# A list schedule with a model of the port that VectorE and GpSimd share, a table of shifts on its priorities, later constants, fewer weight tiles decoded early

## The chip, the core and the metric

The kernel runs on one NeuronCore of a Trainium2 chip. Its engines are TensorE (PE in the profile; PEld is its loading of weights), VectorE (DVE), ScalarE (ACT), GpSimd (POOL) and SyncE (SP), which here issues nearly all DMAs. The metric is the device time of one execution in microseconds (us), as the median of several runs.

## The reference

Three blocks follow one another: causal attention with a decay made from a cumulative sum of log f, a gated feed-forward block with a convolution of width 3 along the sequence, and a Fourier mixing block with a feed-forward network.

```python
# attention: B, H, S, D = 4, 8, 576, 64
cum = np.cumsum(np.log(np.clip(f, 0.0001, 1.0)), axis=-1)
scores = scale * q @ k.T + cum[..., :, None] - cum[..., None, :]     # causal, then softmax
x = softmax(scores) @ v                                              # -> (B, S, 512)
# gated block, d_ff = 1024
h = np.maximum(x @ w_in, 0.0)
conv_out = sum(conv_w[k] * hp[:, k:k + S, :] for k in range(3))      # hp: h padded
x = h * sigmoid(conv_out) @ w_out
# mixing block, hidden width 2048
u = x + np.real(np.fft.fft(np.fft.fft(x, axis=1), axis=2))
un = (u - mean(u)) / np.sqrt(var(u) + 1e-06)
out = u + np.maximum(un @ w_ch1, 0.0) @ w_ch2
```

## The kernel before

Everything is fp32. Where precision is wanted at the speed of float32r, a tensor is kept as a high part (ScalarE copies it to float32r) and a low part (GpSimd or VectorE subtracts, a tensor_tensor), and a product is three matmuls. The weights of the three feed-forward matrices arrive as 64-bit numbers and are decoded to fp32 on the chip: one DMA, an absolute value on ScalarE, a clamp on GpSimd (tensor_scalar) and three bit instructions on VectorE, each over 128x512 (`decode`).

The program is recorded first and ordered afterwards. `build` calls the engines' methods, and each call becomes an `Op` with an engine, a modelled cost in ns (`cost_of`), its predecessors and a priority. `Plan.order` then runs a list schedule over all operations forward (`forward`) and backward (`backward`) in turns; the backward run gives the next priorities, and the best of 40 forward runs is taken. `walk` does the scheduling: each engine takes the ready operation of the lowest priority number. The result is one fixed order of instructions for each engine's queue. In the forward run, TensorE's cost doubles in a stretch of 3413 ns whose predecessor had little work in it, and each DMA occupies a modelled wire. A VectorE instruction of over 32 elements with no PSUM operand is charged `1.25 * c + 60`, whatever GpSimd does.

What is recorded, with tile names as the profile has them:

- Attention, steps s = 0 to 16, two heads a step: scores into PSUM (psatt_s), VectorE adds the mask (att_t, att_nb), ScalarE takes the exponential, TensorE transposes (psatt_u, att_pt), the sums' reciprocals go through DRAM and come back spread over the partitions (att_r, att_rt, att_rb), and the product with v is scaled by them (att_xr), and split into bc_xs. The v tiles are att_tv.
- The gated block of each batch is queued when its 4 steps are through, and filled in between the attention's steps: 8 chunks x @ w_in with the convolution on VectorE (glu_cv__157 and glu_cv__158, three 128x576 instructions a chunk), then 16 chunks with w_out, whose tiles come from DRAM into two buffers (bc_wo__133, bc_wo__134). The result goes to DRAM as z (dram_t__341 to 344, one for each batch).
- The DFT of each batch (dft_*, psdft) reads z and the constant matrices dd (dft_t__3762) and ds (dft_t__3763). These are staged: GpSimd's queue copies the inputs in_dd and in_ds to dram_t__379 and dram_t__380 as float32r by four DMAs, not before a time `hold` in the plan (`1e4 * SCST` ns, 160 us); `load_consts` then loads them from there on SP.
- The last feed-forward block runs in eight passes over four groups of rows and eight groups q of the hidden width, each with the weights of a slot k = q % 5 (mr_*, ml_t, bc_*; products in psc_c). It needs w_ch1 and w_ch2 in 16 tiles each. `NST` of each are decoded during the attention (steps x = 10 on) and stored to DRAM (dram_t__347 on, two for a tile number fo); the rest stand in the list `todo`, of which `decode_some(2)` takes two a step in the third and fourth pass. `stored` loads a decoded tile back (wprep_dw), and `load_pair` makes a slot's weights from four of them: q = 4, the fifth slot, from fo = 8 and 9, in the third pass. All these tiles go through rings of two buffers (wprep_dr, wprep_dw, wprep_de).

An instruction's line in the profile is that of the emitter, so tiles tell the instructions apart, not lines.

Of the kernel before, what the change touches and what calls it, by code (L numbers as in the profile page):

```python
# [200 lines left out]

ENGINES = ("PE", "DVE", "ACT", "POOL", "SP")
# [53 lines left out]
    return n * 0.9 + 30.0  # L256


class Plan:
# [1192 lines left out]
```

## Time and profile before

| | us |
|---|---|
| median of 3 runs (867.5 to 869.25) | 868.6 |
| the profiled execution | 873.15 |
| its span, from the first to the last instruction | 871.4 |
| TensorE busy | 828.5 (95%) |
| VectorE busy | 652.9 (75%) |
| ScalarE busy | 430.2 (49%) |
| GpSimd busy | 250.7 (29%) |

The profile is of one execution. Busy time counts an engine's instructions; neighbours in one queue can overlap a little. The windows give the same for a stretch of the span, with the clock that TensorE was granted in it (1.00 is 2.4 GHz, 0.50 is 1.2 GHz) and the mean share of time in which the 16 DMA engines were busy. The timeline puts instructions in order of time; in square brackets stands an engine's idle time before the instruction and what ended it. A wait for several things is put down to the one that came last.

### The profile page before, as it was taken

What the parts mean: (1) busy time and instruction counts of PE and PEld (TensorE: products, weight loads), DVE (VectorE), ACT (ScalarE), POOL (GpSimd) and SP (SyncE); (2) the same over time, 40 slices, a digit from 0 to 9 for tenths busy, and PEclk for the clock granted to TensorE, in tenths of its full rate; (3) what the DMA queues carried; (4) which work ended last, traced back from release to release, by engine and by line L of the source; (5) the groups of instructions that cost most, each with busy time, mean ns of one, the idle gap of its engine ahead of it and who ended that gap; (6) DMA issues with size and microseconds to landing.
All of it is one profiled execution on the core that took longest, in us unless ns stands there. A gap on an engine that the chain in (4) does not pass through costs nothing.

```text
span 871.4 us, 15330 instructions
## 1 busy us (share of the span) xinstructions
PE 828.5 (95%) x5424; PEld 719.2 (83%) x5424; DVE 652.9 (75%) x1596; ACT 430.2 (49%) x1043; POOL 250.7 (29%) x271
## 2 busy tenths in 40 slices
PE   8999998799999999989899999999999999999998
PEld 6667777588978888889789788988998889899896
DVE  6988989745896598238867767786787888887754
ACT  5988787545775385236534434344432452323220
POOL 2243535400351133229945541232012220000000
PEclk9999999999998999999989999999999999999999
DMA  6464465978446923696886845423265623443222
GB/s 219 152 199 143 156 206 155 326 216 282 133 140 174 316 74 103 207 310 165 203 231 168 205 135 125 142 78 121 87 182 122 178 78 107 118 122 98 73 74 84
DMA packets 97804, 139.61 MB, mean 160 GB/s; under 512 B 17048, under 2 KB 59832, under 8 KB 97728
## 3 DMA queue, kind: packets, MB, share of 16 engines
...
q0 software_dynamic: 576, 2.95, 0.9%
...
## 4 chain that ended last, share of the span: by engine, by line
PE 66%; DVE 15%; DMA 6%; ACT 6%; issue 3%; POOL 3%; SPq 1%; DVEq 0%; ACTq 0%; POOLq 0%
PE psc_c__4874 L511 9%; PE psc_c__4873 L511 9%; PE psbc_bc__556 L511 6%; PE psbc_bc__557 L511 6%; PE psdft_x__3869 L511 4%; PE psdft_x__3870 L511 4%; PE psc_c__5047 L511 4%; PE psc_c__5046 L511 3%; PE psc_c__5045 L511 3%; PE psc_c__5044 L511 3%; DVE glu_cv__158 L511 3%; PE psatt_s__170 L503 3%; DVE glu_cv__157 L511 3%; PE psatt_u__174 L503 2%; PE psatt_u__174 L511 2%
## 5 line engine op out<-in xcount | busy, mean ns | idle before, releaser
L511 ACT ACTIVATE bc_xs__131<-ml_t__5369 128x320 fp32r<-128x320 f32 (+1 forms) x78 | 35.1, 450 | 98.4 <-DVE ml_t__5369 L511 87.3
L511 PE MATMUL psbc_bc__556<-bc_xs__131,bc_wi__130 128*128 128x288 f32 x384 | 62.8, 302 | 1.8 <-ACT glu_t__138 L511 0.8
L511 PE MATMUL psbc_bc__557<-bc_xs__131,bc_wi__130 128*128 128x288 f32 x384 | 62.1, 301 | 0.5 <-DVE glu_t__140 L511 0.5
L511 DVE TENSOR_TENSOR ml_t__5369<-psc_c__4874,ml_t__5369 128x320 f32<-128x320 f32 (+1 forms) x91 | 40.9, 461 | 26.2 <-PE psc_c__4874 L511 25.2
L511 DVE TENSOR_TENSOR ml_t__5369<-psc_c__4873,ml_t__5369 128x320 f32<-128x320 f32 (+1 forms) x91 | 41.0, 461 | 25.4 <-PE psc_c__4873 L511 23.0
L511 PEld LDWEIGHTS psbc_bc__556<-bc_xs__131,bc_wi__130 128*128 128x128 f32 x384 | 53.2, 188 | 3.7 <-ACT glu_t__139 L511 1.0
L511 PEld LDWEIGHTS psbc_bc__557<-bc_xs__131,bc_wi__130 128*128 128x128 f32 x384 | 54.6, 190 | 1.2 <-DVE glu_t__140 L511 0.7
L511 POOL TENSOR_SCALAR wprep_dw__125<-wprep_dw__125 128x512 f32<-128x512 f32 x24 | 17.9, 748 | 104.5 <-ACT wprep_dw__125 L511 104.4
L511 DVE SCALAR_TENSOR_TENSOR bc_xs__131<-ml_t__5369,bc_xs__131 128x320 fp32r<-128x320 f32 (+1 forms) x78 | 38.8, 499 | 10.6 <-ACT bc_xs__131 L511 10.2
L511 POOL TENSOR_SCALAR wprep_dw__122<-wprep_dw__122 128x512 f32<-128x512 f32 x24 | 16.6, 691 | 73.2 <-ACT wprep_dw__122 L511 73.1
L511 DVE COPY glu_t__140<-psbc_bc__557 128x256 f32<-128x256 f32 (+2 forms) x48 | 9.9, 261 | 35.4 <-PE psbc_bc__557 L511 31.9
L511 DVE SCALAR_TENSOR_TENSOR glu_cv__157<-glu_t__138,bc_cw__132,glu_cv__157 128x576 f32<-128x576 f32 x32 | 32.7, 1021 | 1.4 <-ACT glu_cv__157 L511 1.2
L511 DVE SCALAR_TENSOR_TENSOR glu_cv__158<-glu_t__139,bc_cw__132,glu_cv__158 128x576 f32<-128x576 f32 x32 | 31.3, 979 | 2.8 <-ACT glu_cv__158 L511 2.7
L511 ACT ACTIVATE glu_t__140<-psbc_bc__556 128x256 f32<-128x256 f32 (+2 forms) x48 | 8.5, 251 | 45.6 <-PE psbc_bc__556 L511 40.8
L511 ACT ACTIVATE ml_t__5371<-ml_t__5369 128x320 fp32r<-128x320 f32 (+1 forms) x26 | 11.7, 449 | 35.1 <-DVE ml_t__5369 L511 29.0
L503 PE MATMUL psatt_s__171<-att_t__67,att_t__66 64*128 64x288 f32 (+2 forms) x48 | 26.6, 553 | 0.0
L503 PE MATMUL psatt_s__170<-att_t__67,att_t__66 64*128 64x288 f32 (+2 forms) x48 | 26.1, 545 | 0.0
L503 PE MATMUL psatt_u__174<-att_pt__101,att_tv__92 128*64 128x448 f32 (+3 forms) x80 | 21.6, 417 | 1.7 <-ACT att_pt__102 L511 1.6
L503 PE MATMUL psatt_s__172<-att_t__67,att_t__66 64*128 64x288 f32 (+2 forms) x48 | 21.8, 460 | 0.0
L503 PE MATMUL psatt_s__173<-att_t__67,att_t__66 64*128 64x288 f32 (+2 forms) x48 | 21.7, 459 | 0.0
L503 PE MATMUL psatt_u__174<-att_pt__102,att_tv__93 128*64 128x448 f32 (+3 forms) x80 | 21.6, 417 | 0.0
L503 PE MATMUL psatt_s__170<-att_qk__70 64*128 64x288 f32 (+2 forms) x48 | 19.1, 484 | 1.8 <-DVE att_nb__95 L511 1.8
...
## 6 DMA issues: line engine op xcount, KB each, us to landing
wprep_dr__124<-in_moe_w_ch_dram SPq DMA_DIRECT2D x16, 512.0 KB
wprep_dr__121<-in_moe_w_ch_dram SPq DMA_DIRECT2D x16, 512.0 KB, 5.2
bc_wo__133<-dram_t__340 SPq DMA_DIRECT2D x13, 512.0 KB, 4.2
bc_wo__134<-dram_t__340 SPq DMA_DIRECT2D x13, 512.0 KB, 4.1
...
dram_t__346<-mr_us__4906 SPq DMA_DIRECT2D x18, 256.0 KB, 3.6
```

What stands on the lines that cost most here:

```text
L503: getattr(eng[op.eng], f)(**{k: v.real() if isinstance(v, View) else v for k, v in kw.items()})
L511: getattr(eng[op.eng], op.fn)(**kw)
```

## The change

Four things change. `SCST` goes from 16 to 30: the copies of dd and ds are recorded 7 steps later and held to 300 us of the plan instead of 160. `NST` goes from 10 to 8: 8 tiles of each matrix are decoded during the attention, and fo = 8 and 9 of both join the head of `todo`, which grows from 12 to 16. In the forward run a VectorE operation that `two_reads` picks out (no PSUM operand, over 32 elements, neither memset nor reciprocal) is charged its bare cost, and if a GpSimd tensor_tensor is running when it starts, 0.8 of what is left of that. And `order` runs 53 rounds, takes the last one's priorities, whatever span they gave, and adds to each a number of the table SHIFT: 7577 letters, one for an operation in the order of recording, each standing for -31 to +31 us of the plan's time (a lower number goes first).

```diff
-NWO, NST = 2, 10
+NWO, NST = 2, 8
...
-SCST = 16
+SCST = 30
...
+ROUNDS = 53
+LETTERS = "ABCDEFGHIJKLMNOPQRSTUVWXYZabcdefghijklmnopqrstuvwxyz0123456789+-"
+SHIFT = """
+BSSSSzeZSZ89LigeKBR0aZhwnRmwGp--4-+6++mq-s06+-F-8-6u-alusvgW+66w8ulcpbqmiXV+RBCsuVT+UXRzudhlCz99-BsL23wSPSJBIX
...
+"""
...
+def two_reads(fn, kw):
+
+    v = [x for x in kw.values() if isinstance(x, View)]
+    if fn in ("memset", "reciprocal") or "PSUM" in [x.t.slot.pool.space for x in v]:
+        return False
+    return max(x.free() for x in v) > 32
...
+            o.pair = o.eng == "DVE" and two_reads(o.fn, o.kw)
...
+            if o.eng == "POOL" and o.fn == "tensor_tensor":
+                port.append((t, t + o.took))
+            elif o.pair:
+                o.took = (o.cost - 60.0) / 1.25
+                for a, b in port[-8:]:
+                    if a <= t < b:
+                        o.took += (b - t) * 0.8
+                        break
...
-        best = None
-        for k in range(self.rounds):
-            span = self.forward(prio)[0]
-            if best is None or span < best[0]:
-                best = (span, prio)
+        for _ in range(ROUNDS):
+            self.forward(prio)
             prio = self.backward()
-        self.span, out = self.forward(best[1])
+        for i, c in enumerate("".join(SHIFT.split())):
+            prio[i] += 1e3 * (LETTERS.index(c) - 32)
+        self.span, out = self.forward(prio)
```

## Rows read from the trace of the kernel before

**Rows 1.** The page's parts 1 and 4: busy time, and shares of the last chain.

```profile
PE 828.5 (95%) x5424; PEld 719.2 (83%) x5424; DVE 652.9 (75%) x1596; ACT 430.2 (49%) x1043; POOL 250.7 (29%) x271
...
PE 66%; DVE 15%; DMA 6%; ACT 6%; issue 3%; POOL 3%; SPq 1%; DVEq 0%; ACTq 0%; POOLq 0%
```

**Rows 2.** The view of the cores: span in us, mean granted TensorE clock.

```profile
core 0: 871.4 us, clock 0.982
```

**Rows 3.** Windows: length, busy us of each engine (instructions), granted clock, DMA share, GB/s.

```profile
160.00:180.00 20.00, 14.17 (x99) 12.06 (x100) 10.79 (x30) 6.94 (x24) 3.89 (x4) 0.83 0.90 312
0.00:160.00 160.00, 146.98 (x1103) 110.96 (x1103) 142.07 (x435) 128.43 (x358) 66.09 (x83) 0.98 0.57 178
220.00:345.00 125.00, 119.68 (x898) 108.34 (x900) 101.27 (x203) 82.28 (x198) 41.99 (x34) 0.97 0.49 158
300.00:340.00 40.00, 38.86 (x298) 35.90 (x297) 35.83 (x60) 30.75 (x71) 13.55 (x11) 1.00 0.33 103
400.00:500.00 100.00, 92.19 (x584) 83.12 (x583) 76.28 (x154) 48.77 (x97) 65.25 (x72) 0.95 0.76 195
500.00:870.00 370.00, 365.13 (x2044) 323.96 (x2042) 279.12 (x658) 126.22 (x262) 51.49 (x55) 1.00 0.40 114
```

**Rows 4.** TensorE's waits by what ended them: us, times, longest; 29 rows in all.

```profile
PE psbc_bc__556 L511 <- DMA bc_wo__134<-dram_t__340: 5.1, 1, 5.1
...
PE psdft_x__3877 L511 <- DVE dft_ue__3776 L511: 0.2, 1, 0.2
```

**Rows 5.** Timeline: GpSimd's copies, SP's load, the matmul [idle before it and who ended it].

```profile
157.29 1.26 POOL L511 DMA_DIRECT2D dram_t__379<-in_dd_dram  x2
...
160.63 0.73 SPq L511 DMA_DIRECT2D bc_wo__134<-dram_t__340  x1
...
172.24 0.85 PE L511 MATMUL psbc_bc__556<-glu_t__145,bc_wo__134 128*128 128x288 f32 x2 [5.09 <-DMA bc_wo__134<-dram_t__340]
```

**Rows 6.** DMA issues: count, KB each, median us to landing.

```profile
bc_wo__134<-dram_t__340 SPq DMA_DIRECT2D x13, 512.0 KB, 4.1
...
dram_t__346<-mr_us__4906 SPq DMA_DIRECT2D x18, 256.0 KB, 3.6
```

**Rows 7.** Timeline of VectorE, then of GpSimd, around 316 us: start, length.

```profile
314.93 1.91 DVE L511 SCALAR_TENSOR_TENSOR wprep_dw__122<-wprep_dr__121,wprep_dw__122 128x512 int32<-128x512 int32 x1
...
316.76 0.81 DVE L511 SCALAR_TENSOR_TENSOR glu_cv__157<-glu_t__138,bc_cw__132,glu_cv__157 128x576 f32<-128x576 f32 x1
...
317.49 0.61 DVE L511 CUSTOM_DVE_ANT_0 att_t__84<-psatt_s__170,att_t__65 128x448 f32<-128x448 f32 x1
...
314.86 1.42 POOL L511 TENSOR_TENSOR glu_t__150<-glu_cv__158,glu_t__142 128x576 fp32r<-128x576 f32 x1 [2.34 <-issue]
...
316.80 1.24 POOL L511 TENSOR_SCALAR wprep_dw__125<-wprep_dw__125 128x512 f32<-128x512 f32 x1 [0.51 <-ACT wprep_dw__125 L511]
```

**Rows 8.** VectorE's groups by form, 0 to 500 us: count, busy us, mean ns, idle before.

```profile
L511 DVE SCALAR_TENSOR_TENSOR glu_cv__157<-glu_t__138,bc_cw__132,glu_cv__157 128x576 f32<-128x576 f32 x32 | 32.7, 1021 | 1.4 <-ACT glu_cv__157 L511 1.2
...
L511 DVE SCALAR_TENSOR_TENSOR glu_cv__158<-glu_t__139,bc_cw__132,glu_cv__158 128x576 f32<-128x576 f32 x32 | 31.3, 979 | 2.8 <-ACT glu_cv__158 L511 2.7
...
L511 DVE SCALAR_TENSOR_TENSOR glu_cv__158<-glu_cv__158,glu_t__139 128x576 f32<-128x576 f32 x16 | 15.9, 993 | 3.7 <-ACT glu_cv__158 L511 3.5
...
L511 DVE SCALAR_TENSOR_TENSOR wprep_dw__125<-wprep_dr__124,wprep_dw__125 128x512 int32<-128x512 int32 x18 | 15.9, 885 | 0.1
...
L511 DVE SCALAR_TENSOR_TENSOR wprep_dw__122<-wprep_dr__121,wprep_dw__122 128x512 int32<-128x512 int32 x14 | 13.0, 931 | 0.2
```

**Rows 9.** Timeline of SP, then TensorE, around 590 us.

```profile
561.96 0.47 SPq L511 DMA_DIRECT2D wprep_dr__124<-in_moe_w_ch_dram  x1
...
587.56 0.32 SPq L511 DMA_DIRECT2D dram_t__369<-wprep_dw__125  x1
...
592.70 0.32 SPq L511 DMA_DIRECT2D wprep_dw__122<-dram_t__365  x1
...
600.10 0.31 PE L511 MATMUL psc_c__4873<-bc_wi__130,ml_t__5378 128*128 128x320 f32 x1
```

More of the change, by code (lines that the diff above doesn't have):

```diff
@@ new lines @@
+TFBBBFBBBBBBBOBBBFBWSDWBBYeCFLCBbHTLIWSFFLCGUHBECVJCFTBRLEECFYFHFBBBCBDBSJPFJBCIDheZ2oU-FIQf1DCCEWFRNRFJy1vBg+
+4S7aFBQncC6BCD6TSSHBBBmILfBBBQCG0BDBBTB3UGoqlY5BCRlnv+OVIIFLnUhZjEKggbdcpgdpYsqbmtshrqutqt439Yp--VNdXUIRmkebqc
+6+qT1+x+foRQhWz1i7B63358wbGHEjOMpjjXbTYNOVPUJgFJefYYHGVeNYoQuiiWviVWaUeehgkmkXlfVirfdcBJCNo3995rmGlbRv30m4sCxs
+07yehhrpjvfeLWeSrdu-eJNBNJYXcSuWHBGr--J--9c-x5--+-0y89--WlmuusbjgnCs85lonsaelr2HkfIGNNGG420qMZOObfQJEQVJELEbcT
+YWZk8+Zihwhfga1sHTQDBBJzZWatjfrLTOUtVtuXPZesSGXaaYWQLQLNhSSDBBl-sq9-pT2mb+Kxg+gr+TVHqxi+OQBxix0VdSeXUfUiHBB36-
@@ new lines @@
+v8+-8--zz+894+8890SMTVQPGaIBBDGeMBLSCBIGBlaEUd401HbpDBCGPRVHMNMRBDFRIIwBH-IXJeYsBQCGcCEcKJ0ez1qDcLSSUEDEBBGHFG
+JGaKCUhcBOMyJwqeJ2YjVOOUTJ770BBBBBBCCCBBGLMNTCDJBZKBC-DDfJYSS3BBz+v0-GQNSNegafcYVPhPMbgLo-dBEtEY0PGJDZq75nEBJK
+WQHCBBBCBBBBBBBBBBDBBBBCDJNBBBCBCFYFBBBDDBDcMCB755EJDEaQUYnbEDWp7giDUVOENbaEdOagd1ih0hNu-sluoRXXWfYocgamOCDDDD
+QVHBBCFFBLGRFFBHCDGFDDDHEJy7qkcUCBDEFBBBI3-neBNIZX8pZZGu4N41zvLD2x-zz1533-g4KLC+-c6IJIjhHhDBRp35uDBNYHNTKdQYKG
+INELFGhnNNwor83ku-GlSmmkOmROOTYGdLELMUeEBLClvBh72moMLKK---uBCCoy88fBBBCCBCYBJPiGQXVedRVGJBBBCDBCKHPBIJNuNKU99B
@@ new lines @@
+cBBICBBHJJHOHHNKKIhHHHHHOLTJLWM5XIILCBBBBHFBHJNIQSgaBBiFLkIRCFFHCDDBBNFBBFWPlqoCELgTcwUUTRhsmhBtUNCCLGIGDgHDI1
+immsqZFrbIcvgtWNGNIMJLdJLUWULLIHIahYUReeidiiaYeklHfwFROGQsBgjepWOHEEBC6IOTWYYFHEGIaRSBLFBFgCBBDBBBFUeKPDDPBJFG
+BNBBFPKYPQWHZlYo0ut-+5+----9---9v-gQoIGFKFGMQF3HBBBBhWBHBEFBKBbcBBBBBBFBDBDNCBBcKCSKx-w5GBBbgbhfnjj4zx1xhpPgtg
+1WNfgalwdZBBCCFQHI-3-9UurEMFbt253yMXCLPbTTv231-6J2++6+5vo-EYs3pq8nNsNOlZZIBei1peIBBOBBBBBBBBBBCLBeN-+-dZ4zFCet
+9--nWZpaarZWatjjiqSypFgpt889Tn38BN2fCBkoiGNaSMBBH-kolFZI2QzUX7ejj4TUhH6730P4xcoVBJBBEDCJKBNDvbbecMBEBDCQJjMgUX
@@ new lines @@
+5Xa-+-s4-suo6i267kijfjodZtg-+8-lv91---69-T++lgSKSoFEQQ+586tpg5x8vYbLvXmJaYmRkuEIEKRQPWbUMutb--4IK3SHadEBPBa---
+Hy-Vck+7wnfhfKURSvEFxtLTOGdvp-yjpu4xVcrjaTNFUJ1+-SSe2+++NTf2YWLVUgr58-r+o+z862-r-t9Kv3-j0-8--aXR9i49q4+7-8826w
+47+-wvfzCInnnpnXIRJPNYgODgFMbg5wlFk7qkZXSxR7k5etkK3+IFnlWn3k1djiwkfjF-mjsiUjLSWZraECDFFPFDFEDBJCEDBGBGBBBJBJBB
+BPIOdZqidjfZmml2zzbTimlMnpEWWjFDpaex8H7v59wztwhY4tV72BBBq0BDMdxLjUj33bJDIaUJTQaJEZBcfBBwVtqTweP3+urrlr8k1ukBL4
+BMl1BVBCHBIBFMaFJo5MGfBu34i8z62k7wjrloBMUrJBBjEeXTUhJedmSFQIFBCCBGCOCBBBBBJEa-7x-+-seJJJXYYwM-fWvhcc-0aa-inSd-
@@ new lines @@
+KKamWil--WpF9Z2xg88hT2jJFHEFFEIJNWQHJWSDDMMEUEK1HXmbotDnrz-kqtiEFIRBSlnBBBBYMSGBBZBBDC--dgXR--Y-Z-Phd75xxrq2V4
+o9B56ySukjljoEDCBBBBG0+TUodjOBaQcFBNsZOS-9gYPZ52--xf6TKWBiJq-cHlhv-7vsD0Wm0zqqZyTSSYBCj3lVgnPv-s-w---uln3-3---
+-f9oD9n19frRhCiKverUpfKLQMIaNcZ9bJGZY+-REFBK648vDWggSTNRwKRr0--4skhhx3coOmw2pwVal+Wu-G8F+4-CUOhIdJJJJJKJJJJJJJ
+JJJJJJHJJJJJJJJJJIIJIRI+8+eBBoenmlSvECFOQ-FLGQfqgUIrbxThTReNI03k2ao-80+EPaObhB6mfmuBNBBOWilkyTCSkbIan0BZXEBBTu
+NIORNTQRTdbmldlgjQBw7ftq5YxsgvaLDLDBMOfhxwlROB--3cj5i49++-Bq198----88p8ObXaaXvwyogMJtjsnQr+d+4-+9+99----4lyhbp
@@ new lines @@
+wZxHat5edt5ut7OxguMsJMDUGIIIQjIFmoIYduggmlUVPOCTTacXYMKXonqBBBcjcdnfWFHMMOLNCDLlMNUabxnXLavdfBycN-LpGkIlNLGbeI
+LBFDKDGHCBBOwRfohlhNLKJQLPIPNLFZDBHDFJEIBCBBBBXRKMBBBBWhBEDDEGBBBBDUi+XNrntpjsJQLVidSqp1+09++87Xw0uQVkLFEQLDNH
+HK7bSfZVwUVgsYITcwLr4Ke7mdCZPBMGmr17sgYtrlehlaeMLHZWYm5452aqoneq4r-iUMKGDRaYfsyETBbkajJs88h97-9+-9++7+8-6779+8
+87e4ObzcquW53N+-+---+-6suoUYjdX-----------9-6-12lXSSUpyVEBqEVdziDIMgVY540tsDqpo23KK2Zj7dw2vr-ts--PYvBrVWcQRFRB
+Bkr-hq-0iZJo7uiY0-woYTMKTzddDHTDHMDFYHZddjsmXUODHdrs0wZV3eBBQERRXBMBXfnRqk1powrfZO-ZZgZumkbWUbufVw--jww77v7-Hu
@@ new lines @@
+aex07BRMeGpGNW0IMDb+mbZ-9lqdZ5RkowrooB001MXBBBQcLBr9Pqh--ayw5ykhJqh16-5188q7z02EFrqWfdsHoBHMYVDGIezKETDmmtXHea
+NDhoYZZTrakuh8mz3efphwVxrz8NG1zxq5SkJZ399kp+Z-4x45vf6qqnzMp2aRWpCDRpcUXnoIqJORJOlJCKHNQRLJJSJ-8-HtPWowWnNjMBBJ
+MGMDJIBagixenjhFNzkdmXStrUQ-7UroWfsro-7WezgYYo2bkzdhdl+2exrqe-7B6ijfV3z27BROUjZMpNLJFONLcY9vr33jTp3KsDUgIDT0-+
++c1H7BEc6azj8fC-hFuREu-as40--wstrw889367+825+7T1-lvvjhc9Y-6qy8gRpqXBSobIENGhke58QQwrfGY97p4bM3o8one3zmNohfolZx
+BqYBBvB98KH7-923-8-433+5W9575y67-68t13l-56aR-95wO-in40u-j26TC1m7m35s-+--5-nX0ECi-U39dX9m64+----r2-p---79-ueqOg
@@ new lines @@
+NLy3Uw05dkjIBFGgTgMShXjgiGeroM-kuFknvkEBRWQ3WNXPjBCPGY3KWmHCBCERvLBGBDBDBEZh6+-hh56479w-+6-+q86dmX-8nmqySDcq-z
++FTNEgBCBBBCBBTB-+v8-v6wpBTfj6FgsQ5yv-69---1-MGRBCPGFJnBBDCGEv5p7174-46ikn0gIHcIBB1DQROFDBxejXhffNqPKBBBBZzBB3
+zr6E-3-vrPnjjneWmIHEBdmuRIMOB9hw-GDBijDITYO5Jvm-uCktcU2XyBGuBKCLDCDHtkgquj-y-yHmiQKXcKBBCdf7ZcBNBCKSFIldcQPOBS
+OcaJBDBBBDBBO2UlhPejy0kfYvgtdZZCCCCCCMtBBPaniBVg-LbiizfjSzXefb+rvhxvhrrqmslrkPtQHJp-YVodeyyuc31LWFcJBO6jiINMIt
+XLYuWEpJsbXZ1dlfUCBFHCBBDFbhCEFF9dYaVO8glV-7bcVm+f6o99-fhfb1yJJLeYLrjBg306dUChfYQHJnqkf3rj----j72c-3--z6s-413B
@@ new lines @@
+Ib-8-97-v2-0--MWlSe+mieWYrBply2iabByphiCBBndeYhpsRnurtUkT3BBvukeKBBPBBEDBDKBNEOP5OBjVbIEYjCEjzImKratZnfxikz14M
+8CMBSWB+CobtRReBPIcDL7qMx7Ti-TK-KfUGMGoKSDEeEjOBIFDBCGBFFJJChBHFfRfNwdRqgNNXTo7X6X7-k766BlLnQghOYECMfiQXLBBBEf
+kbYPs767v2-U9bLd1yL8gaZTmb7+Z34-Uu4d8924vkPPDDBCNBCCCDBCGGCNXBDDIDBDBBEX+rEJJCr8v9tj--9z--9tl3cz688152r0aZ1hu0
+hEbblcBeRXQyCrVMBCHXBCLKoLBBCOBqPTYhRMMXVejYtrOOKe7336Yj71ypxwWa5qWfgdB7E+4yrz8++Bg3+++f++8+92l9894960699+69+9
+TYifefeBMgHdo3qgoSWuh0i88+7-Y1-y-c-idBBCCD9GMRCJLD9vtMdymnKELVEVOQiJGJGNBBhEQiWSQEXf44uQluj--RX0h7tpQm4KQBbEat
@@ new lines @@
++3198vW0y7+t7Empw0t6z-5-------7yoYSu1dm43x37685887+tvw4-llhhiizs-------7---9999-7-64z5wr--zZX104xo86pH+9lX-p8-
+3+k4-6--v++++m7---7++nt7Bhon-668211+W044-2K-Wlol7+qL-zz9+1LnVpwwyBbwCFRBEMCJ-DUBIkmjt93--7xmy-6y17--+--+--+---
+-------7---300p+ery-gf6i7NOHN9997-2q-y76-+y3-lzhm3hm9----c-8WkrfX2t8-fjoXo2NX918577--8-XoSVVXgdiUSJkokktmil---
+---44WDDEDDWDXJEEBCEFFQampsxgwdy------0++9-8+8--9++-++-------4------+9-------+------+------++7-------+0-------
++t-------------790y8-y--55yxw2uz2-1-lmklmltommn7mm5lyfyrBBCBT9-13z0tk2v2k6MDmBnpy3+glkpuOqof2ro4x
@@ L198 @@
 class Op:
-    __slots__ = ("eng", "fn", "kw", "subs", "cost", "preds", "pools", "prio", "lead", "hold", "end", "work", "took", "late")
+    __slots__ = ("eng", "fn", "kw", "subs", "cost", "preds", "pools", "prio", "lead", "hold", "end", "work", "took", "late",
+                 "pair")
 ENGINES = ("PE", "DVE", "ACT", "POOL", "SP")
@@ L266, in __init__ @@
         self.begin = {"PE": 0.0, "DVE": 600.0, "ACT": 600.0, "POOL": 1600.0, "SP": 600.0}
-        self.bias, self.lead, self.hold, self.rounds = 0.0, 0.0, 0.0, 40
+        self.bias, self.lead, self.hold = 0.0, 0.0, 0.0
     def pool(self, name, space="SBUF", side="left", after=()):
@@ L416, in forward @@
     def forward(self, prio):
-        ops, busy = self.ops, {}
+        ops, busy, port = self.ops, {}, []
         wire = [0.0]
```

18 lines of the change are left out of this document (added).

## The prediction

> **What bounds the kernel now.** I read the page's busy times and chain first. TensorE is busy in 95% of the span and holds 66% of the chain that ended last, VectorE 15% [rows 1]; the row of the core adds a granted clock of 0.982 [rows 2]. The windows, read as a stretch less PE's busy time in it, then show two kernels. From 500 us on TensorE waits 4.9 us in 370, at full clock, with VectorE at 75%: nothing that reorders the other engines can shorten that much. Before 160 us it waits 13.0 us, and VectorE is busy for 142 of the 160; from 220 to 345 it waits 5.3 us with VectorE at 101 of 125; from 400 to 500, 7.8 us [rows 3]. So what an order can win lies in the first 500 us. The list of TensorE's waits names who ended them: 29 rows, 38.1 us together, of which VectorE ends 17.1, ScalarE 10.8, DMA 9.1 and GpSimd 1.1 [rows 4]. The longest is one wait of 5.1 us for a tile of w_out. A clock of 0.982 over 871.4 us is a further 15.7 us of lost TensorE time. Waits and clock, some 54 us, are all that there is to gain.
>
> **The constants (SCST 16 to 30).** Before, GpSimd issues the copies of dd and ds from 157.29 us on. The w_out tile issued on SP at 160.63 us lands for the matmul at 172.24, ahead of which TensorE idled 5.09 us [rows 5]; the median of the 13 loads of that buffer is 4.1 us to landing [rows 6]. From 160 to 180 us the granted clock is 0.83, which means the 1.2 GHz level for a third of those 20 us, and costs 20 x 0.17 = 3.4 us; the DMA engines are 90% busy there, while VectorE has 10.8 and ScalarE 6.9 us of work in the 20 [rows 3]. So no other engine was in the way, and I put 5.1 + 3.4 = 8.5 us down to the copies. The change lets them go from 300 us of the plan on. From 300 to 340 us the DMA share is 0.33 and TensorE waits 1.1 us [rows 3]: the copies find free engines, though v tiles, the reciprocal rows of the softmax (att_rb), z rows and w_ch tiles pass there too. The price at the new place lies between nothing and the same 8.5 us; I take 1.5, near the free end, because the share there is about a third of that at the old place. Sum: -7.0. The copies' one reader, the first DFT's loads, comes after the third batch's convolution has begun; if they were late for it, TensorE would wait one for one.
>
> **Eight tiles a matrix early, not ten.** Four decodings (of each, one DMA in, one ScalarE, one GpSimd and three VectorE instructions, one DMA out) leave the stretch before 345 us for the lists of the third and fourth pass. SP issues the eight DMAs there among those of the passes, and VectorE has a quarter of its time free [rows 3]: four tiles of about 2 us are 8 us out of some 90 free ones, so I cost the work at nothing. What is not free is their date, which is a rival below. Where they leave, TensorE waits little, so I book no gain either.
>
> **The port.** The plan charged each VectorE instruction with SBUF operands 25% and 60 ns more, always; now it charges the bare cost, and 0.8 of what is left of a GpSimd tensor_tensor that runs when it starts. The rows bear this out. A 128x512 instruction at 314.93 under a GpSimd tensor_tensor from 314.86 took 1.91 us and ended 0.56 us behind it; a 128x576 one at 316.76 took 0.81 us under a GpSimd tensor_scalar, and the next started 0.73 us after it had [rows 7]. The change's bare cost of the latter is 576/0.96 + 68 + 61 = 729 ns; the old cost was 971. So both cases are now in the plan, and it can put long VectorE work beside other GpSimd work. A bare length in the trace is that cost and the 0.08 us by which neighbours overlap: 810 ns for this form, 748 without the pointer's 61, and 512/0.96 + 68 + 80 = 681 for the decoding. The means are 1021 and 979 (32 each), 993 (16), 885 (18) and 931 (14) [rows 8]: 6.8 + 5.4 + 3.9 + 3.7 + 3.5 = 23 us of stretching in these five groups. A new order avoids something between none and all of it; I take half, 11.6 us, since dependencies don't let the two engines be kept apart everywhere. It shortens the run only where VectorE sets the pace, by the rows 0 to 160 and 220 to 345 us, 285 of the first 500 [rows 3]: 11.6 x 285/500 = 6.6 us. The waits left for an order are 38.1 - 5.1 = 33.0 us; 6.6 is 20% of them, and as the low clock follows waits I take 20% of the clock's other 12.3 us as well, 2.5. Sum: -9.1.
>
> **The table and the 53 rounds.** Each of 7577 operations has its priority moved by up to 31 us of the plan's time, over a base that is the 53rd round and no longer the best of 40. It adds no instruction. No row tells its sign by itself: at best it is worth all 33.0 + 12.3 = 45 us of waits and clock, at worst it makes a new stall. I count it as what makes the 9.1 us come about, and leave its failures to the rivals.
>
> [...]
>
> **The sum.** The profiled execution took 873.15 us, 1.75 of it around its span of 871.4; 873.15 - 7.0 - 9.1 = 857.05. The median of the runs shown is 4.55 us lower, so 868.6 - 16.1 = 852.5.
>
> **The rivals.** First the forecast, 0.47; its own range is 845 to 861, from the port's gain and the copies' price between a half of what I take and double of it. Second, the order wins far more: half of the 45 us above, so 868.6 - 7.0 - 22.6 = 839. For it, VectorE and ScalarE end 28 of the 38 us of waits; against it, most of the 29 are single links of under 2 us between stages. 0.13. Third, only the constants count, and the order wins here what it loses there: 868.6 - 7.0 = 861.6. For it, the last round's priorities need not be the best, and a fixed order is as good as its landing times, one of which was 11.6 us against a median of 4.1 [rows 5, 6]. 0.15. Fourth, the change doesn't do what it says: at 300 us the copies hit the next w_out tiles as they did at 160, and the order washes out: 868.6. Against it the share of 0.33 [rows 3]. 0.07. Fifth, slower: the moved tiles come late. The weights in the fifth slot, made of two of them, feed TensorE from 600.10 us on. In the order of before, the third tile of the late list, which would now be one of these, is loaded at 561.96 and stored at 587.56, 25.6 us later; the load that fetches it for the slot goes out at 592.70 [rows 9]. A store of this size lands in 3.6 us [rows 6], so the slack is 592.70 - 587.56 - 3.6 = 1.5 us. If the list runs no earlier than it did, each us of lateness beyond is one of TensorE, up to a whole turn of 25.6, with 3.4 us of low clock behind it as at 172 us: 868.6 - 16.1 + 25.6 + 3.4 = 881.5. It decides the sign from a wait of some 16 us on. Against it, the plan knows the dates and VectorE has room from 500 us on. 0.18.
>
> **How the numbers follow.** Faster by over 0.2% (1.7 us, about what a measurement of this kernel can tell from no change) are the first three, less 0.01 of the third: 0.74. Within it: 0.08. Slower: 0.18. The range takes in the second to the fourth and the smaller part of the fifth: 838 to 873.
>
> **What would show it.** Right: no TensorE wait on w_out between 155 and 180 us, and full clock there; the copies in a stretch of low DMA share, with no wait on att_rb or w_out behind them; means of the five groups of [rows 8] nearer to 810, 748 and 681 ns; under 10 us of TensorE's idle time before 160 us. Wrong: groups as long as before (then the order didn't work by the port), a wait on the fifth slot's weights near 600 us (the slower rival), or more than 6 us of idle time from 500 us on (the moved work isn't hidden).

## The result and the profile after

The changed kernel takes 856.1 us in the median (855.1 to 857.4), the kernel before 868.9 beside it: a ratio of 0.985, interval 0.982 to 0.988. The forecast was 852.5, its own range 845 to 861. The profiled execution took 855.14 us, 1.7 of it around the span.

The page's parts 1 and 4 of the changed kernel, and its row in the view of the cores:

```profile
PE 821.7 (96%) x5424; PEld 710.6 (83%) x5424; DVE 651.7 (76%) x1596; ACT 432.8 (51%) x1043; POOL 250.1 (29%) x271
...
PE 70%; DVE 13%; ACT 8%; POOL 4%; issue 3%; DMA 2%; SPq 0%; DVEq 0%; ACTq 0%; POOLq 0%
```

```profile
core 0: 853.4 us, clock 0.994
```

Against [rows 1, 2] the span is 18.0 us shorter. TensorE's busy time fell by 6.8 us for the same 5424 matmuls, with a better clock (0.982 to 0.994); its idle time, span less busy, fell from 42.9 to 31.7, by 11.2. VectorE's work is the same within 1.2 us. DMA holds 2% of the chain in place of 6%. The profiled execution of before lies 4.2 us above that kernel's median, so the two profiles are 18.0 us apart where the medians are 12.8; the ledger below follows the profiles.

The windows of the changed kernel (length, busy us of PE, PEld, DVE, ACT and POOL with instructions, granted clock, DMA share, GB/s):

```profile
0.00:160.00 160.00, 145.07 (x1085) 110.08 (x1085) 136.21 (x417) 126.00 (x346) 66.73 (x80) 0.97 0.56 175
160.00:180.00 20.00, 18.49 (x148) 15.17 (x147) 17.04 (x59) 13.66 (x45) 4.85 (x5) 1.00 0.85 277
220.00:345.00 125.00, 123.04 (x958) 109.27 (x957) 90.35 (x196) 76.01 (x193) 38.82 (x32) 1.00 0.52 162
300.00:340.00 40.00, 40.00 (x313) 36.01 (x313) 27.09 (x56) 26.75 (x66) 13.83 (x12) 1.00 0.46 138
400.00:500.00 100.00, 95.62 (x590) 83.72 (x588) 80.37 (x169) 44.99 (x87) 63.52 (x78) 1.00 0.82 213
500.00:840.00 340.00, 338.05 (x1903) 298.97 (x1902) 266.34 (x633) 121.04 (x252) 43.44 (x46) 1.00 0.42 121
```

Beside [rows 3]: from 160 to 180 us TensorE's idle time went from 5.8 to 1.5 us and the clock from 0.83 to 1.00. From 300 to 340, where the copies now run, TensorE never waits, with a DMA share of 0.46 for 0.33. From 220 to 345 it idles 2.0 us for 5.3. But before 160 us it idles 14.9 us, more than the 13.0 of before, although VectorE has 6 us less to do there.

TensorE's waits after, the first rows and the last of 24:

```profile
PE psbc_bc__554 L601 <- ACT glu_t__138 L601: 2.2, 3, 1.2
PE psbc_bc__554 L601 <- ACT glu_t__148 L601: 2.1, 2, 1.3
PE psc_c__4743 L601 <- DVE ml_t__5380 L601: 1.9, 3, 0.8
...
PE psc_c__5051 L601 <- DVE dft_ue__3805 L601: 0.2, 1, 0.2
```

No DMA ends one any more; in [rows 4] DMA ended 9.1 of 38.1 us. The 24 rows hold 27 us.

**A ledger of the gain.** The count of matmuls that TensorE has started by a given time shows where one kernel gets ahead of another. It is the PE count of a window that begins at 0. The kernels' orders differ, and a count weighs long and short matmuls alike, so a lead of a few matmuls means little. c1, c2 and c12 are experiments of the next section.

| by (us) | before | c1: only the copies moved | changed | c2: copies put back | c12: without the table |
|---|---|---|---|---|---|
| 160 | 1103 | 1103 | 1085 | 1088 | 1128 |
| 200 | 1360 | 1424 | 1387 | 1318 | 1435 |
| 345 | 2412 | 2481 | 2494 | 2425 | 2545 |
| 500 | 3382 | 3434 | 3482 | 3422 | 3494 |
| 800 | 5017 | 5081 | 5137 | 5063 | 5170 |

The changed kernel is 18 matmuls behind at 160 us, 82 ahead at 345, 100 at 500 and 120 at 800. Its gain lies from 160 to 500 us, and the first 160 us cost some of it.

### The profile page after: what moved, and what is told of

Read it like the earlier page. It is cut to its first block, busy times and chain, and to the rows that moved or that the text cites. A ratio compares the mean times of both kernels' runs of the same rounds, so it can differ in the third digit from the quotient of the medians.

```text
span 853.4 us, 15323 instructions
## 1 busy us (share of the span) xinstructions
PE 821.7 (96%) x5424; PEld 710.6 (83%) x5424; DVE 651.7 (76%) x1596; ACT 432.8 (51%) x1043; POOL 250.1 (29%) x271
## 4 chain that ended last, share of the span: by engine, by line
PE 70%; DVE 13%; ACT 8%; POOL 4%; issue 3%; DMA 2%; SPq 0%; DVEq 0%; ACTq 0%; POOLq 0%
PE psc_c__4743 L601 10%; PE psc_c__4742 L601 10%; PE psbc_bc__554 L601 8%; PE psbc_bc__555 L601 7%; PE psdft_x__3934 L601 5%; PE psdft_x__3935 L601 4%; PE psc_c__5054 L601 4%; PE psc_c__5053 L601 4%; PE psc_c__5051 L601 3%; PE psc_c__5052 L601 3%; PE psatt_u__174 L593 2%; DVE glu_cv__158 L601 2%; DVE glu_cv__157 L601 2%; PE psatt_s__170 L593 2%; PE psatt_u__174 L601 2%
## 5 line engine op out<-in xcount | busy, mean ns | idle before, releaser
L601 PE MATMUL psbc_bc__554<-bc_xs__131,bc_wi__130 128*128 128x288 f32 x384 | 68.3, 304 | 2.7 <-ACT glu_t__138 L601 2.2
L601 PE MATMUL psbc_bc__555<-bc_xs__131,bc_wi__130 128*128 128x288 f32 x384 | 67.2, 304 | 0.3 <-ACT glu_t__139 L601 0.3
L601 PEld LDWEIGHTS psbc_bc__554<-bc_xs__131,bc_wi__130 128*128 128x128 f32 x384 | 55.6, 189 | 5.1 <-ACT glu_t__138 L601 2.9
L601 PEld LDWEIGHTS psbc_bc__555<-bc_xs__131,bc_wi__130 128*128 128x128 f32 x384 | 55.7, 190 | 1.2 <-ACT glu_t__139 L601 0.5
L601 DVE TENSOR_TENSOR ml_t__5380<-psc_c__4743,ml_t__5380 128x320 f32<-128x320 f32 (+1 forms) x91 | 40.6, 459 | 15.9 <-PE psc_c__4743 L601 14.0
L601 POOL TENSOR_SCALAR wprep_dw__125<-wprep_dw__125 128x512 f32<-128x512 f32 x24 | 18.5, 771 | 114.6 <-ACT wprep_dw__125 L601 114.6
L601 DVE SCALAR_TENSOR_TENSOR glu_cv__157<-glu_t__138,bc_cw__132,glu_cv__157 128x576 f32<-128x576 f32 x32 | 32.3, 1009 | 11.2 <-ACT glu_cv__157 L601 10.9
L601 POOL TENSOR_SCALAR wprep_dw__122<-wprep_dw__122 128x512 f32<-128x512 f32 x24 | 17.9, 746 | 56.6 <-ACT wprep_dw__122 L601 56.6
L593 PE MATMUL psatt_s__171<-att_t__67,att_t__66 64*128 64x288 f32 (+2 forms) x48 | 25.4, 530 | 0.0
L593 PE MATMUL psatt_s__170<-att_t__67,att_t__66 64*128 64x288 f32 (+2 forms) x48 | 25.4, 529 | 0.0
L593 PE MATMUL psatt_u__174<-att_pt__101,att_tv__92 128*64 128x448 f32 (+3 forms) x80 | 24.0, 452 | 0.4 <-ACT att_pt__102 L601 0.4
L593 PE MATMUL psatt_u__174<-att_pt__102,att_tv__93 128*64 128x448 f32 (+3 forms) x80 | 24.0, 452 | 0.0
L593 PE MATMUL psatt_s__173<-att_t__67,att_t__66 64*128 64x288 f32 (+2 forms) x48 | 20.9, 442 | 0.0
L593 PE MATMUL psatt_s__172<-att_t__67,att_t__66 64*128 64x288 f32 (+2 forms) x48 | 20.8, 439 | 0.0
L593 PE MATMUL psatt_u__169<-att_pt__101,att_tv__99 128*64 128x448 f32 (+4 forms) x72 | 19.3, 413 | 1.2 <-ACT att_pt__102 L601 1.2
```

What stands on the lines that cost most here:

```text
L593: getattr(eng[op.eng], f)(**{k: v.real() if isinstance(v, View) else v for k, v in kw.items()})
L601: getattr(eng[op.eng], op.fn)(**kw)
```

## The experiments

The theory is the prediction's: the copies' old place costs some 7 to 8.5 us, and the rest of the gain comes because the plan knows the port, with the table as its means. (The port is the plan's name for the stretching of VectorE's instructions beside GpSimd's; the runs show the stretching, not what lies behind it.) The rivals: the copies are all of it; the order wins by something other than the port; the table does harm.

**1. Only the copies, in a fixed order.** The order of before (or of the changed kernel) is worked out in full, and then the four copies of dd and ds alone are moved in GpSimd's queue. Nothing else is planned anew.

```diff
 seq = self.order()
+copies = [i for i in seq if self.ops[i].eng == "POOL" and self.ops[i].fn == "dma_start"]
+seq = [i for i in seq if i not in copies]
+at = next(k for k, i in enumerate(seq) if self.ops[i].eng and self.ops[i].end - self.ops[i].took >= 3e5)
+seq[at:at] = copies
```

Before, with its copies at 300 us of the plan:

> The order of before, untouched but for GpSimd's four copies of dd and ds, which are taken out of its queue at 157 us and put back behind the work planned before 300 us. If the forecast's first term holds, the wait of 5.1 us on w_out at 172 us and the low clock behind it go and at most 1.5 us come back: 868.9 - 7.0 = 862, between 860 and 865. Rival: the w_out loads are late anyway, for the two buffers, or the copies cost the same at 300 us: 868 to 870.

Measured: 862.5 us, ratio 0.991 (0.9876 to 0.9943), 8.6 us less (5 to 11 by the interval). Windows of this kernel:

```profile
160.00:180.00 20.00, 19.73 (x160) 15.58 (x162) 13.63 (x46) 13.99 (x45) 4.05 (x4) 1.00 0.82 280
300.00:340.00 40.00, 38.24 (x292) 33.44 (x291) 34.64 (x58) 28.80 (x66) 17.86 (x16) 1.00 0.52 162
0.00:200.00 200.00, 186.54 (x1424) 144.63 (x1426) 168.09 (x529) 154.40 (x440) 70.01 (x87) 0.98 0.61 194
```

The wait on w_out and the low clock of [rows 3, 5] are gone, and at the new place TensorE idles 1.8 us in 40 against 1.1 before. In the ledger c1 equals before at 160 us, is 64 matmuls ahead at 200, 52 to 69 ahead after that and 64 at 800: the gain is made in those 40 us and kept.

The changed kernel's order, with the copies put back to 160 us (the same edit with 1.6e5):

> The order of the changed kernel, untouched but for the four copies, which go back to where 160 us is planned. If the copies cost 8.5 us wherever they meet the w_out loads: 856.1 + 7 = 863. Rival: the new order asks for its w_out tiles so early that the copies find slack: 856 to 858.

Measured: 866.0 us, ratio 0.9942 (0.9922 to 0.9962) to before. The changed kernel's two ratios are 0.985 and, measured again in experiment 2, 0.9829, so the copies put back cost 8 to 10 us of 871.1. But the wait isn't on w_out this time. The timeline of this kernel on GpSimd, SP, ScalarE, VectorE and TensorE (start, length, in brackets the idle time before and who ended it):

```profile
161.80 1.26 POOL L605 DMA_DIRECT2D dram_t__373<-in_dd_dram  x2
...
165.59 0.89 SPq L605 DMA_DIRECT2D wprep_dr__124<-in_moe_w_ch_dram  x1
...
180.08 0.66 ACT L605 ACTIVATE wprep_dw__125<-wprep_dr__124 128x512 f32<-128x512 f32 x1 [8.61 <-DMA wprep_dr__124<-in_moe_w_ch_dram]
180.64 0.37 ACT L605 ACTIVATE att_pt__101<-psatt_u__174 128x256 f32<-128x256 f32 x1
...
181.04 0.42 DVE L605 COPY att_pt__101<-psatt_u__174 128x256 f32<-128x256 f32 x1 [7.34 <-ACT att_pt__101 L605]
...
181.52 0.69 PE L605 MATMUL psatt_u__174<-const_t__61,att_t__84 128*128 128x128 f32 x2 [5.11 <-DVE att_pt__101 L605]
```

Read upwards: TensorE idles 5.11 us for a copy out of PSUM on VectorE; that shares its tile with one on ScalarE, and ScalarE stands 8.61 us at the head of its fixed queue for a raw weight tile that nobody needs for long. That load took from 165.59 to about 180.1, 14.5 us. In the changed kernel the same load is read 7.5 us after its issue (timeline of SP and ScalarE):

```profile
165.16 0.44 SPq L601 DMA_DIRECT2D wprep_dr__124<-in_moe_w_ch_dram  x1
...
172.70 0.69 ACT L601 ACTIVATE wprep_dw__125<-wprep_dr__124 128x512 f32<-128x512 f32 x1 [0.57 <-DMA wprep_dr__124<-in_moe_w_ch_dram]
```

So the copies' price isn't tied to the w_out tile: in either order a load that went out beside them came late, and what stood behind it in some engine's order paid. In these two fixed orders the place at 160 us costs 8.6 and 8 to 10 us. It isn't a price of the place alone: c4 of experiment 3, another order, sends the same copies out at 161.62, and there TensorE idles only 0.6 us at full clock (window of c4):

```profile
160.00:180.00 20.00, 19.38 (x164) 16.29 (x160) 11.24 (x36) 9.83 (x30) 4.89 (x7) 1.00 0.98 339
```

**2. Without the table.** All else as changed; the last round's priorities are used as they are.

```diff
-for i, c in enumerate("".join(SHIFT.split())):
-    prio[i] += 1e3 * (LETTERS.index(c) - 32)
```

> The changed kernel without the table: 53 rounds, their last priorities, no shifts. If the table carries the order's part of the gain, it goes: 856.1 + 5.8 (12.8 measured less the constants' 7.0) = 862, and the plan's own spans (831.6 without, 824.5 with the table) say + 7.1 = 863. Rival: the table only fits the plan's errors, and the charge for the port, the tiles and the constants bring the gain: 855 to 858.

> The changed kernel without the table once more, on the same chip as the changed kernel. If the table is worth nothing on the chip and this order is one of the better draws: 848 to 851, and 5 to 9 us below the changed kernel, with intervals that don't meet. If the earlier 849.0 was the chip's state: 855 to 858, as the changed kernel.

> The changed kernel once more, beside the next one on the same chip. By its runs so far ratio 0.985, 855 to 858.

Measured: 849.0 us (ratio 0.9752, 0.9707 to 0.9796), and again 849.5 (0.975, 0.9717 to 0.9784). In that second comparison the changed kernel itself gave 855.9 (0.9829, 0.9795 to 0.9863); the intervals don't meet. On the chip the table costs 6.4 us. The plan's own span says the opposite: 831.6 us without it, 824.5 with it. By the ledger the loss is there by 160 us (1085 matmuls for 1128) and stays near it until 345 (2494 for 2545). At 7.6 matmuls per us, the changed kernel's pace from 160 to 345, 43 matmuls are 5.7 us. At 500 us only 12 matmuls of the lead are left, at 800 us it is 33; what gives them back and takes them again stays open.

Two places before 160 us show how such time is lost. The first, in the timeline of the changed kernel on SP, ScalarE, VectorE and TensorE:

```profile
45.44 0.33 SPq L601 DMA_DIRECT2D wprep_dr__121<-in_moe_w_in_dram  x1
...
52.06 0.66 ACT L601 ACTIVATE wprep_dw__122<-wprep_dr__121 128x512 f32<-128x512 f32 x1 [1.37 <-DMA wprep_dr__121<-in_moe_w_in_dram]
52.63 0.37 ACT L601 ACTIVATE att_pt__102<-psatt_u__174 128x256 f32<-128x256 f32 x1
...
53.03 0.42 DVE L601 COPY att_pt__102<-psatt_u__174 128x256 f32<-128x256 f32 x1 [0.95 <-ACT att_pt__102 L601]
...
53.51 0.66 PE L601 MATMUL psatt_u__174<-const_t__61,att_t__79 128*128 128x128 f32 x4 [1.32 <-DVE att_pt__102 L601]
```

This is the chain of c2 in small: a raw tile lands 1.37 us after ScalarE has come to it, and the copy out of PSUM behind it comes late for VectorE and for TensorE. The second, on GpSimd, VectorE, ScalarE and TensorE:

```profile
139.09 0.73 POOL L601 TENSOR_TENSOR wprep_de__123<-wprep_dw__125 128x255 f32<-128x255 f32 x1 [2.92 <-DVE wprep_dw__125 L601]
139.77 1.42 POOL L601 TENSOR_TENSOR bc_xs__131<-att_xr__69,bc_xs__131 128x576 fp32r<-128x576 f32 x1
...
139.19 0.65 DVE L601 TENSOR_SCALAR wprep_de__123<-wprep_dw__125 128x2 f32<-128x2 f32 x1
139.75 0.41 DVE L601 COPY att_pt__102<-psatt_u__169 128x256 f32<-128x256 f32 x1
140.09 1.38 DVE L601 TENSOR_TENSOR wprep_de__123<-wprep_dw__125 128x255 f32<-128x255 f32 x1
...
141.55 0.63 ACT L601 ACTIVATE wprep_dr__121<-wprep_de__123 128x512 fp32r<-128x512 f32 x1 [3.30 <-DVE wprep_de__123 L601]
142.09 0.58 ACT L601 ACTIVATE att_pt__101<-psatt_u__174 128x512 f32<-128x512 f32 x1
...
142.72 0.55 PE L601 MATMUL psatt_u__174<-const_t__61,att_t__83 128*128 128x128 f32 x3 [1.71 <-ACT att_pt__101 L601]
```

VectorE's instruction at 140.09 stands in the plan with 0.49 us and took 1.38: on the chip it falls under a GpSimd tensor_tensor which in the plan starts after it, and the plan charges only for one that already runs. ScalarE stands idle for 3.30 us until its result is there, and the copy out of PSUM behind that comes late for TensorE. What precedes and follows each of the two, in the windows of the changed kernel:

```profile
50.00:54.00 4.00, 2.02 (x15) 1.32 (x14) 3.05 (x11) 2.24 (x6) 0.61 (x1) 1.00 0.41 116
54.00:62.00 8.00, 7.29 (x35) 3.50 (x35) 4.32 (x14) 5.27 (x16) 2.54 (x2) 0.57 0.39 126
139.00:143.00 4.00, 1.73 (x12) 1.28 (x13) 4.00 (x12) 1.45 (x4) 2.84 (x3) 1.00 0.40 131
143.00:147.00 4.00, 4.00 (x21) 3.37 (x19) 1.96 (x11) 3.99 (x14) 3.08 (x3) 0.57 0.39 130
```

In the 4 us before each stretch TensorE was busy for 2.02 and 1.73 us. Then the granted clock is 0.57, at 0.50 for most of it (54.43 to 61.25 and 143.18 to 146.59 us): 8 x 0.43 + 4 x 0.43 = 5.2 us of lost TensorE time, about all that a clock of 0.994 leaves over the span. In c12 the clock from 0 to 160 us is 0.99, here 0.97. So in these two places lateness of about a microsecond (waits of 1.32 and 1.71 us), which the plan doesn't know, was paid as a wait and again in the clock. In experiment 4 the same order without GpSimd's tensor_tensor has made the early loss up by 160 us, which fits the clash as its cause; the order without the table wasn't run that way, so why the table's is the more exposed of the two is argued, not shown.

**3. Is it the port charge?** One kernel has the new charge alone (copies at 160 us, ten tiles early, best of 40 rounds, no table); one has the old charge with the copies at 300 us and eight tiles early (best of 40); one has the old charge in the changed kernel without the table; and two are the changed kernel without the table in other rounds.

```diff
-SCST = 16
+SCST = 30
...
-NWO, NST = 2, 10
+NWO, NST = 2, 8
...
-            if o.eng == "POOL" and o.fn == "tensor_tensor":
-                port.append((t, t + o.took))
-            elif o.pair:
...
-ROUNDS = 53
+ROUNDS = 55
```

(c10 is the first two hunks on the kernel before; c9 is the third on the kernel of c12; c7 is the fourth there, and c8 with 52; c4 is the changed kernel with the first two undone, and the loop of before.)

> The kernel before with the new charges of VectorE's instructions alone: constants at 160 us, ten tiles early, best of 40 rounds, no table. If the port's charge makes the order (the forecast's second term): 868.9 - 9.1 = 860. By the plan's own spans (841.4 before, 836.3 so) 864. Rival: the order keeps its stretched VectorE instructions, as the changed kernel's trace does (99 us of stretching by overlap against 102 before), and the charge alone is worth nothing: 867 to 871.

> A second order with the old charges: the kernel before with the constants at 300 us and eight tiles a matrix early, planned anew, best of 40 rounds. Same theories, same numbers: 861 to 864 if the port's charge counts, 849 to 861 if it doesn't.

> The no-table kernel of the 53rd round with the old charges of VectorE's instructions, constants and tiles as changed. If the port's charge is worth the 6 to 9 us of the forecast, an order without it stands that much above the three orders with it (849.0, 855.4 and 860.9, mean 855.1, ratios 0.975 to 0.988): 861 to 864, ratio near 0.99 as when the constants alone were moved. Rival: the constants and the lottery of orders are all: 849 to 861, ratio 0.975 to 0.988.

> The changed kernel without the table, with the priorities of the 55th round instead of the 53rd. The plan says 835.2 for it, 831.6 for the 53rd round (848.98 on the chip, so 17.4 above the plan), 836.2 for the port's charge alone (857.1, 20.9 above). If an order without the table stands 17 to 21 us above its plan, and the table's (824.5 planned, 856.1 measured, 31.6 above) is the odd one: 852 to 856. Rival: orders differ on the chip by chance, whatever the plan says, and the 53rd round was a lucky one: anything from 848 to 870, without relation to the plan.

> The same with the priorities of the 52nd round, of which the plan says 843.6. If the distance to the plan is 17 to 21 us without the table: 861 to 865. Rival, chance: anything from 848 to 870.

Measured, each ratio against the kernel before in the same comparison; the plan's spans are its own numbers, and spans under different charges aren't comparable:

| kernel | charge | copies, tiles early | priorities of | plan's span | chip, us | ratio (interval) |
|---|---|---|---|---|---|---|
| before | old | 160, 10 | best of 40 | 841.4 | 868.9 to 871.6 | 1 |
| c4 | new | 160, 10 | best of 40 | 836.2 | 857.1 | 0.9844 (0.9796, 0.9892) |
| c10 | old | 300, 8 | best of 40 | 842.3 | 858.7 | 0.9855 (0.9813, 0.9896) |
| c9 | old | 300, 8 | round 53 | 840.1 | 849.1 | 0.975 (0.9704, 0.9797) |
| c12 | new | 300, 8 | round 53 | 831.6 | 849.5 | 0.975 (0.9717, 0.9784) |
| c8 | new | 300, 8 | round 52 | 843.6 | 855.4 | 0.9808 (0.9772, 0.9845) |
| c7 | new | 300, 8 | round 55 | 835.2 | 860.9 | 0.9877 (0.9832, 0.9922) |
| changed | new | 300, 8 | round 53 and table | 824.5 | 855.9 | 0.9829 (0.9795, 0.9863) |

With the same round and no table, old and new charge give the same time. Rounds 53 and 55 of one plan differ by 11 us (c12 and c7), and the plan's span doesn't rank the five orders made with the new charge: its shortest is third of them on the chip, its longest second. c4 alone gains 14.0 us, c10 alone 11.4, and both with the table 12.8: edits that plan anew don't add up. Each is another draw of an order, and the draws lie between 849 and 861 us. In c4's draw the copies at 161.62 cost next to nothing (experiment 1; of its 1.4 us of waits on w_out only 0.2, at 178 us, lie near them), so c4 is no measure of the charge either. Two or three draws of a kind don't settle whether the new charge moves the middle of that scatter by a few us; that stays open.

**4. What the port itself costs.** In both kernels every GpSimd tensor_tensor becomes two tensor_scalar instructions over the same tile, in the same fixed order. They copy the second operand, so sums, products and the low parts of the split weights are left out.

```diff
+if op.eng == "POOL" and op.fn == "tensor_tensor":
+    for _ in range(2):
+        nc.gpsimd.tensor_scalar(out=kw["out"], in0=kw["in1"], scalar1=1.0, scalar2=1.0, op0=ALU.mult, op1=ALU.mult)
+    continue
```

> The order of before, with each GpSimd tensor_tensor replaced by two tensor_scalar copies of its later operand, which take about as long and by the rows don't stretch VectorE; the low parts and sums are thus left out of the result. It prices the port as a whole in that order. The forecast took half of the stretching in five groups, 11.6 us, for 6.6 us of the run; all of it would be some 13 us, so 869 - 13 = 856. Rival: what VectorE gains is hidden behind TensorE, 866 to 870. Second rival: it is worth far more than the forecast took, as the charge alone (857.1 against 871.1) suggests: below 850.

> The same replacement in the order of the changed kernel, with the same work left out. If its order still runs into the port where VectorE sets the pace (99 us of overlap against 102 before), it gains as much as the order of before does, 8 to 13 us: 844 to 848. If the order took its gain by keeping the stretched instructions off the path, less than half of that: 852 to 856.

Measured: before 855.8 us (ratio 0.9815, 0.9776 to 0.9854), 15.9 less; changed 852.2 (0.978, 0.9742 to 0.9819), 4 to 6 less than its own ratios of 0.985 and 0.9829. VectorE's groups by form, 0 to 500 us, of the kernel before without tensor_tensor on GpSimd (count, busy us, mean ns, idle before):

```profile
L516 DVE SCALAR_TENSOR_TENSOR glu_cv__157<-glu_t__138,bc_cw__132,glu_cv__157 128x576 f32<-128x576 f32 x32 | 29.2, 914 | 1.5 <-ACT glu_cv__157 L516 1.2
L516 DVE SCALAR_TENSOR_TENSOR glu_cv__158<-glu_t__139,bc_cw__132,glu_cv__158 128x576 f32<-128x576 f32 x32 | 28.5, 891 | 4.6 <-ACT glu_cv__158 L516 4.4
L516 DVE SCALAR_TENSOR_TENSOR glu_cv__158<-glu_cv__158,glu_t__139 128x576 f32<-128x576 f32 x16 | 15.0, 939 | 5.2 <-ACT glu_cv__158 L516 5.1
L516 DVE SCALAR_TENSOR_TENSOR wprep_dw__125<-wprep_dr__124,wprep_dw__125 128x512 int32<-128x512 int32 x18 | 13.9, 774 | 0.1
L516 DVE SCALAR_TENSOR_TENSOR wprep_dw__122<-wprep_dr__121,wprep_dw__122 128x512 int32<-128x512 int32 x14 | 11.3, 807 | 0.2
```

Over the bare 810, 748 and 681 ns the five groups keep 3.3 + 2.6 + 3.1 + 1.7 + 1.8 = 12.5 of the 23 us of [rows 8]: about half is gone. VectorE's busy time over the whole span fell from 652.9 to 619.0 us. What is left stands beside tensor_scalar, all that the edit leaves of the two forms on GpSimd. The bare lengths are those that the trace of before has where nothing on GpSimd overlaps by over 0.1 us: 0.81 us (27 instructions), 0.75 (14) and 0.69 (73) in the mean. In the kernel before a GpSimd tensor_scalar that started first stretched VectorE from the bare 0.81 to 1.20 us (timeline of GpSimd and VectorE):

```profile
306.40 0.61 POOL L511 TENSOR_SCALAR wprep_dw__122<-wprep_dw__122 128x512 f32<-128x512 f32 x1 [2.58 <-ACT wprep_dw__122 L511]
306.43 1.20 DVE L511 SCALAR_TENSOR_TENSOR glu_cv__157<-glu_t__138,bc_cw__132,glu_cv__157 128x576 f32<-128x576 f32 x1
```

In [rows 7] the same two forms met the other way round: VectorE started at 316.76, 0.04 us ahead of GpSimd, and took its bare 0.81 us, while the tensor_scalar took 1.24 us instead of 0.61. The same groups of the changed kernel, with its tensor_tensor in place:

```profile
L601 DVE SCALAR_TENSOR_TENSOR glu_cv__158<-glu_t__139,bc_cw__132,glu_cv__158 128x576 f32<-128x576 f32 x32 | 32.6, 1018 | 4.6 <-ACT glu_cv__158 L601 4.3
L601 DVE SCALAR_TENSOR_TENSOR glu_cv__157<-glu_t__138,bc_cw__132,glu_cv__157 128x576 f32<-128x576 f32 x32 | 32.3, 1009 | 11.2 <-ACT glu_cv__157 L601 10.9
L601 DVE SCALAR_TENSOR_TENSOR glu_cv__158<-glu_cv__158,glu_t__139 128x576 f32<-128x576 f32 x16 | 16.0, 997 | 2.7 <-ACT glu_cv__158 L601 2.7
...
L601 DVE SCALAR_TENSOR_TENSOR wprep_dw__125<-wprep_dr__124,wprep_dw__125 128x512 int32<-128x512 int32 x16 | 12.3, 771 | 0.2
...
L601 DVE SCALAR_TENSOR_TENSOR wprep_dw__122<-wprep_dr__121,wprep_dw__122 128x512 int32<-128x512 int32 x12 | 10.4, 868 | 0.2
```

They hold 6.7 + 6.4 + 4.0 + 1.4 + 2.2 = 20.7 us: 2.6 less than before. The decodings hold 3.6 less, in part because 4 of their 32 instructions now come after 500 us; the three groups of the convolution hold 17.1 us for 16.1. So the clash is worth more than the prediction gave it, and the change avoids little of it. Where the same clash is taken out of the changed kernel, only 4 to 6 us come back. The first window of that kernel (c6):

```profile
0.00:160.00 160.00, 147.13 (x1126) 111.50 (x1128) 133.88 (x442) 131.07 (x367) 69.09 (x121) 0.99 0.58 187
```

By 160 us TensorE has started 1126 matmuls for 1085, level with the order without the table (1128). At 345 us the lead is 64 (2558 for 2494), at 500 us only 14 (3496 for 3482). So without GpSimd's tensor_tensor the table's early loss is gone; what holds this order up from 345 us on wasn't tried.

## Why the prediction was right, and where it was wrong

**The sign and the range.** 856.1 lies in the forecast's own range, 3.6 us above its 852.5. The two terms missed in opposite directions: against 868.9 the run gained 12.8 us where 16.1 were summed; the constants gave 8.6 instead of 7.0, the rest 4.2 instead of 9.1. Each ratio's interval is some 3 us either way, so the 4.2 is rough: by the ratios (0.991 for the copies alone, 0.985 and 0.9829 for the whole change) it is 5 to 7. That the sum came so near is partly luck, since the larger term came about in another way than the one that it was worked out from. The range isn't the one that its sentence describes either: half and double of the two terms make 843 to 859, and 856.1 lies in that too.

**The constants: right.** The old place was put at 8.5 us, and two fixed orders give 8.6 and 8 to 10. The new place was bounded by nothing and 8.5 and taken at 1.5; the rows say near nothing. In the changed kernel the copies go out here (timeline of GpSimd):

```profile
311.50 1.26 POOL L601 DMA_DIRECT2D dram_t__373<-in_dd_dram  x2
312.75 1.03 POOL L601 DMA_DIRECT2D dram_t__374<-in_ds_dram  x2
```

and TensorE is busy for all of 300 to 340 us. What the step didn't see is that the victim is the order's: a w_out tile in one, a raw w_ch tile in another, and hardly any in c4.

**Eight tiles early: no cost seen, a gain overlooked, not measured alone.** The fifth rival's date was met. The tile that was to decide it, in the timeline of SP after:

```profile
541.65 0.45 SPq L601 DMA_DIRECT2D wprep_dr__124<-in_moe_w_ch_dram  x1
...
566.35 0.32 SPq L601 DMA_DIRECT2D dram_t__359<-wprep_dw__125  x1
...
573.08 0.32 SPq L601 DMA_DIRECT2D wprep_dw__122<-dram_t__359  x1
```

Its turn from load to store is 24.7 us, as in [rows 9], but it begins 20 us earlier, and the slack is 573.08 - 566.35 - 3.6 = 3.1 us. From 500 to 840 us TensorE idles 2.0 us, and none of its waits is on a slot of weights. But the step booked no gain, and the windows suggest one. From 220 to 345 us VectorE's instructions on the decoded tiles (wprep_dw) take 20.3 us for 32.0 before, which is all of the 10.9 us by which its work there fell (101.3 to 90.4); TensorE's idle time in that stretch went from 5.3 to 2.0 us. A kernel with ten tiles in the changed order wasn't tried, since it needs a new plan, and that is a new draw.

**The port: the step that failed.** It was built of two factors. The first, that a new order avoids half of 23 us, measured 2.6. The second, that half shortens the run by 6.6 and gives back 2.5 of clock, measured 15.9 when about half was really taken out (10.8 us of it in the five groups), beside 33.9 us less of VectorE's busy time in all: other VectorE instructions were relieved too, which the prediction's sum left out. And its reading of [rows 7] was wrong: the plan's new charge counts a tensor_scalar as free for VectorE, while what told the two cases apart is which engine started first. In the trace of before, 29 instructions of the convolution and the decodings were overlapped, by over 0.1 us, only by a GpSimd instruction that started after them, and none is more than 0.01 us over its bare length. Those that started under one that already ran, and met no other, are longer by 0.64 us (23 under a tensor_tensor) and 0.20 us (8 under a tensor_scalar) in the mean. The errors partly cancel, and none is what made the run faster: the text's own sign, groups as long as before, says that the order didn't work by the port, and c9 reaches the time of c12 without the new charge. What the order did win stands in the ledger. Against c1 the changed kernel is 37 matmuls behind at 200 us, 13 ahead at 345, 48 at 500: it loses 37 / 7.6 = 4.9 us early, wins 50 / 7.6 = 6.6 from 200 to 345, and 35 more by 500 at 6.4 per us there, 5.5. The sum, 7.2, is near the distance of the two profiled spans (860.8 and 853.4). TensorE's idle time, window less busy time, splits much the same way: 17.1 us for c1's 13.5 up to 200 us, 2.0 for 6.2 from 200 to 345, 6.2 for 12.2 from 345 to 500. VectorE's instructions of the convolution aren't shorter; from 220 to 345 us fewer decodings lie among them. How much of these wins is the eight tiles' and how much the draw's stays open: c9, c10 and c12 have eight tiles as well, and c4 shows that an order with ten can win as much.

**The table: wrong sign.** It was counted as what makes the port's gain come, with its failures left to the rivals. It costs 6.4 us, most of it there by 160 us, where the text wanted under 10 us of idle time and 14.9 were measured (13.3 without the table).

**The rivals.** The third, the order winning here what it loses there, is nearest in mechanism: true before 200 us, but its 861.6 leaves out some 12 us won later. The second, an order that wins far more, wasn't this one, but the round without the table goes part of the way to it: 849 us, better than both kernels.
